# Keys' maxima by a product with the identity, large px in quarters, and one more step in each attention unit, in a fused attention and MoE kernel

## The chip, the cores and the metric

One core of a Trainium2 chip runs the program. The metric is the time of one execution on the device in microseconds; less is better.

## The reference

Linear attention with two softmaxes, then a feed-forward layer with a hard swish. Batch 8, 8 heads, 576 tokens, head size 64; 4608 tokens of 512 features in all, hidden size 2048; everything is float32.

```
q_s = softmax(q, over the 64 features);  k_s = softmax(k, over the 576 tokens)
kv  = k_s^T v                 # 64 x 64 for each batch and head
x   = q_s kv                  # tokens x 512 when the heads stand side by side
h   = x @ w_in;  g = h * clip(h + 3, 0, 6) / 6;  out = g @ w_out
```

## The kernel before

The 4608 tokens are three blocks of 512 ("block 0, 1, 2") and three large blocks of 1024 ("large block 0, 1, 2"). Heads are taken in four pairs `hp`. Each float32 factor of the big products is split into two parts, hi and lo (`split`, L119: a cast on ScalarE, a subtraction on VectorE), and a product is made of three.

**Blocks.** For each of the 16 chunks of the hidden size, `gemm1` makes 12 matmuls of 512 columns (`ph`), `relu6` and `split` make its `g`, and `gemm2` of the chunk before follows, 12 matmuls into four accumulators (`po`). `store` (L701) sends a block's result through the ring of tiles `v`. In block 0 the weights are decoded (`decode`).

**Sums of weights.** The large blocks use a scheme of seven products instead of eight, which needs sums of weight blocks. `sum_weights` (L426) makes four of them for each of 8 pairs of chunks and both sides, so 16 times, one yield or two each, during blocks 1 and 2. The four sums stand in one tile `v`, their hi and lo parts go into two tiles of the ring `gp`, and from there to DRAM (`keep`).

**Large blocks.** `factors(s)` makes the seven right factors from x (L494 on), `phase1` 56 slots of six matmuls into g, `phase2` 56 slots of six for the output. The left factors come from DRAM by `fetch`, through two fixed tiles and the ring `gp` (4 tiles, which `gemm1` uses too).

**Attention.** `token_attention` (L341) is a generator, one per head pair, for block 2 (`block_attention`) and the large blocks (`sb_attention`). Its steps:

1. load q, and for every new batch b: `kt` (keys with features on partitions, one buffer), `ke` (keys with tokens on partitions), `vt`;
2. for every new b the maxima `km` of `kt` (VectorE, L355), spread to 128x128 as `kb` on GpSimd (L357); then q's softmax and its turn into `qT` (`q_softmax_t`; the tile is called m);
3. for every new b: `pm`, a transpose of `kb` on TensorE, so that every row holds the maxima of the keys' features; `ke - pm` (VectorE, L364), its exp (ScalarE);
4. nothing; 5. `kv_of`: ten products of 65 columns, each into one half of the array's columns, give `pkv`, and VectorE makes `kv` from it: 128x128, the two heads on the diagonal, zero elsewhere;
6. for each chunk of 512 tokens `px`: `kv` times `qT`, one product of full size for each batch in the chunk, and a copy into x on ScalarE (L385).

`steps(units, length)` strings the units together: one step per call, a unit's last step behind the first of the next one. The loop over chunks calls it twice a chunk (once for the last two chunks of a block), the large blocks once every two slots. A block's loop runs the attention of the next block, block 2's that of large block 0, and large block s that of s + 1.

`pm`, `pkv` and `px` share two PSUM banks (`bank_a`). From block 1 on TensorE's instructions stay in the order in which the program makes them (`mm`, L85); the other engines' order is the scheduler's, by a timeline of its own. `behind(units)` (L124) makes an exception: what a unit issues comes behind the instructions in `front`, on their engines.

Of the kernel before, what the change touches and what calls it, by code (L numbers as in the profile page):

```python
# [1 line left out]

# [16 lines left out]
P = 128  # L19
# [13 lines left out]
def attention_moe(  # L33
# [88 lines left out]
    front = []  # L122

    def behind(units, count=1):  # L124

        with ExitStack() as order:
            for ins in front:
# [129 lines left out]
    def attention(j, hp):  # L257

        if not j:
            kt, qt, qT, vt, ke = first[hp]  # L260
        else:
            kt, ke, vt = load_k(j, hp)
# [26 lines left out]
    def load_k(b, hp, tokens=False):  # L289
        kt = att.tile([P, S], F32, name="kt", bufs=1)  # L290
        nc.sync.dma_start(kt, kT[b, hp])
        ke = att.tile([P, NCH, P], F32, name="ke", bufs=2)
        if tokens:
            nc.sync.dma_start(ke, k[b, hp].rearrange("p c h d -> p c (h d)"))
        vt = att.tile([P, NCH, 2, D + 1], F32, name="vt", bufs=2)
        nc.sync.dma_start(vt, v[b, hp])
        return kt, ke, vt
# [43 lines left out]
    def token_attention(t0, n, hp, put):  # L341
# [8 lines left out]
        loads = {b: load_k(b, hp, tokens=True) for b in need if (b, hp) not in kvs}  # L350
        yield
        new = {}
        for b, (kt, ke, vt) in loads.items():
            km = att.tile([P, 1], F32, name="km", bufs=2)
            nc.vector.tensor_reduce(km, kt, axis=AX.X, op=ALU.max)  # L355
            kb = att.tile([P, P], F32, name="kb", bufs=2)
            nc.gpsimd.tensor_copy(kb, km.broadcast_to([P, P]))  # L357
            new[b] = ke, vt, kb
        qT = q_softmax_t(qt)
        yield  # L360
        for ke, vt, kb in new.values():
            pm = bank_a("pm")
            flip(pm[:, 0:P], kb)
            nc.vector.tensor_sub(  # L364
                ke, ke, pm[:, 0:P].rearrange("p (o n) -> p o n", o=1).broadcast_to([P, NCH, P])
            )
            nc.scalar.activation(ke, ke, AF.Exp)
        yield
        yield
        for b, (ke, vt, kb) in new.items():  # L370
            kv_of(b, hp, ke, vt)
        yield
        for c in range(n // TB):
            px = bank_a("px")
            at = t0 + c * TB
            for b in need:
                lo, hi = max(b * S - at, 0), min((b + 1) * S - at, TB)
                if lo < hi:
                    mm(px[:, lo:hi], kvs[b, hp], qT[:, c * TB + lo : c * TB + hi], True, True)
            put(c, hp, px)  # L380
        yield

    def sb_attention(s):
        def put(c, hp, px):
            nc.scalar.copy(x_of(s)[:, hp, c * TB : (c + 1) * TB], px)  # L385

        return [token_attention(START + s * SB, SB, hp, put) for hp in (0, 2, 1, 3)]

    def block_attention(j):
        def put(c, hp, px):  # L390
# [35 lines left out]
    def sum_weights(pair, side):  # L426
# [13 lines left out]
        s1, s2, s3, s4 = (sums[:, n * HT : (n + 1) * HT] for n in range(4))  # L440
# [4 lines left out]
        for i in range(2):  # L445
            dst = moe.tile([P, 2, TB], F32R, name="gp", bufs=4).rearrange("p i n -> p (i n)")
            four = dst.rearrange("p (k e n) -> p k e n", k=2, e=2)
            src = sums[:, i * TB : (i + 1) * TB].rearrange("p (k n) -> p k n", k=2)
            split(four[:, :, 0], four[:, :, 1], src)
            for k_ in range(2):  # L450
                block = (S1, S2, S3, S4)[2 * i + k_]
                keep(pair, side, block, dst[:, k_ * TB : (k_ + 1) * TB].bitcast(F32))
# [70 lines left out]
    def relu6(g, r, h):  # L523
        nc.scalar.activation(r, h, AF.Relu, bias=three, scale=1.0)  # L524
        nc.vector.scalar_tensor_tensor(g, r, 6.0, h, op0=ALU.min, op1=ALU.mult)  # L525

    def phase1(s):
        xb, yb, zb = {}, {}, {}
        for i, (p, n) in enumerate(SLOTS1):
# [24 lines left out]
            with tc.high_priority():  # L554
                if n == 1:
                    nc.scalar.copy(h11, x)
# [3 lines left out]
                if n == 3:  # L560
                    nc.scalar.copy(h21, x)
                if n == 2:
                    nc.scalar.copy(h22, y)
                if n == 4:
                    nc.vector.tensor_add(h22, h22, x)  # L565
                if n == 5:
                    relu6(h12, temp(), x)
                if n == 6:
# [3 lines left out]
                    nc.vector.tensor_sub(h12, h22, h12)  # L572
            yield

    def phase2(s):
# [6 lines left out]
        def make():  # L582
# [7 lines left out]
            front[:] = split(t[:, 0], t[:, 1], src)  # L590
# [78 lines left out]
    def gemm1(j, f):  # L669
# [11 lines left out]
        split(gp[:, 0], gp[:, 1], g)  # L681
# [85 lines left out]
    for j in range(NB):  # L767
        if j == 1:
            in_order.append(True)
        if j < NB - 1:  # L770
            turned = (j + 1) * TB >= TURNED
            units = block_attention(j + 1) if turned else [attention(j + 1, hp) for hp in range(NP)]
            step = steps(units, 6 if turned else 4)
        else:
            step = steps(sb_attention(0), 6)
            fac = factors(0)
        chunks = [*range(NFC)] if j < NB - 1 else [NFC - 1, *range(NFC - 1)]
        for n, f in enumerate(chunks):
# [10 lines left out]
            for _ in range((2 if f % 4 == 3 else 1) if not j else 2 if n < 14 else 1):  # L789
# [3 lines left out]
            if j == NB - 1 and n >= 14:  # L793
                for _ in range(3):
                    next(fac, None)
# [7 lines left out]
    with tc.high_priority():  # L803
        for _ in fac:
            pass
        fetch(GROUPS - 2)

    for s in range(NS):
        more = s + 1 < NS
        step = steps(sb_attention(s + 1), 6) if more else iter(())  # L810
# [76 lines left out]
```

## Time and profile before

| | us |
|---|---|
| median of 3 runs (841.83 to 843.0) | 841.92 |
| profiled execution | 839.71 |
| its span in the profile | 837.9 |
| end of block 2, start of large block 0 in it | 346.5 |

TensorE is busy for 96% of the span, VectorE for 81%, ScalarE for 53%, GpSimd for 8%. Times are in us from the start of the span unless ns stands beside them. PE is TensorE, PEld its weight loads, DVE VectorE, ACT ScalarE, POOL GpSimd, SP SyncE. A name like `px<-m,kv` is output <- inputs. A float32 product leaves two records on TensorE, a product of split parts and a transpose one.

### The profile page before, as it was taken

The numbers are of one execution on the slowest core, as the hardware profiler recorded it, in microseconds if no ns is written. First come the engines' busy times: TensorE is split into PE (matmuls) and PEld (weight loads), VectorE is DVE, ScalarE is ACT, GpSimd is POOL, SyncE is SP. The second block draws the span as 40 slices with busy tenths as digits, with TensorE's granted clock in tenths as the row PEclk, the third lists the DMA queues.
The fourth block names the chain that finished last, engine by engine and source line by source line (L and its number), as shares of the span: only waits on it lengthen the run. The fifth ranks groups of instructions, "written<-read, shape, count | busy, mean of one in ns | idle before, by whom it ended". The sixth has DMA issues, their size and how long they took to land.

```text
span 837.9 us, 11778 instructions
## 1 busy us (share of the span) xinstructions
PE 805.7 (96%) x4032; PEld 648.1 (77%) x4032; DVE 677.7 (81%) x1095; ACT 442.4 (53%) x717; POOL 68.0 (8%) x179
## 2 busy tenths in 40 slices
PE   4999989999999999999999999999999999999997
PEld 3677767777887877787877788777888888888886
DVE  7998999999778998579989994698599836558873
ACT  7997764444344454355456653545466535445542
POOL 5000011020100112001112000010000000000000
PEclk9899999999999999999999999999999999999999
DMA  9999676678549661578775577665566775665672
GB/s 362 415 407 319 220 256 208 217 241 288 183 153 357 203 236 51 179 264 292 279 252 184 184 233 254 220 224 162 176 194 188 246 247 187 194 201 187 192 227 98
DMA packets 75643, 192.30 MB, mean 230 GB/s; under 512 B 7232, under 2 KB 19520, under 8 KB 73536
## 3 DMA queue, kind: packets, MB, share of 16 engines
q1 hardware_dynamic: 75008, 190.51, 67.2%
q10 hardware_dynamic: 576, 1.05, 0.4%
q8 instruction: 32, 0.52, 0.3%
q14 instruction: 27, 0.22, 0.1%
HBM read 147.49 MB, written 44.04 MB: 229 GB/s over the span
## 4 chain that ended last, share of the span: by engine, by line
PE 67%; DVE 18%; DMA 5%; ACT 4%; issue 3%; POOL 2%; SPq 0%; ACTq 0%; DVEq 0%; POOLq 0%
PE x L87 30%; PE z L87 12%; PE y L87 11%; PE po L87 6%; PE ph L87 5%; PE px L87 2%; DVE gp L120 2%; POOL swap L312 2%; DVE g L525 2%; PE pkv L87 1%; DVE v L150 1%; DVE v L154 1%; DMA v<-whole 1%; DMA qt<-in_qf_dram 1%; ACT qt L228 1%
## 5 line engine op out<-in xcount | busy, mean ns | idle before, releaser
L120 ACT CAST gf<-g 128x512 fp32r<-128x512 f32 x168 | 104.4, 623 | 95.2 <-DVE gf L120 34.9
L87 PE MATMUL po<-w,gp 128*128 128x512 f32 x576 | 146.5, 400 | 4.1 <-ACT gp L120 3.4
L87 PE MATMUL ph<-x,w 128*128 128x512 f32 x576 | 144.1, 398 | 2.9 <-ACT w L120 2.6
L120 DVE TENSOR_TENSOR gf<-g,gf 128x512 fp32r<-128x512 f32 x168 | 112.9, 685 | 26.2 <-ACT gf L120 25.4
L87 PEld LDWEIGHTS po<-w,gp 128*128 128x128 f32 x576 | 106.3, 189 | 32.4 <-ACT gp L120 6.2
L87 PEld LDWEIGHTS ph<-x,w 128*128 128x128 f32 x576 | 108.7, 190 | 27.8 <-ACT w L120 3.5
L87 PE MATMUL x<-right,gp 128*128 128x512 f32 x384 | 94.9, 392 | 0.4 <-DVE g L565 0.4
L87 PE MATMUL x<-gf,gp 128*128 128x512 f32 x384 | 94.0, 390 | 0.4 <-DVE gf L120 0.4
L87 PEld LDWEIGHTS x<-right,gp 128*128 128x128 f32 x384 | 71.7, 188 | 16.4 <-DVE g L565 0.8
L87 PEld LDWEIGHTS x<-gf,gp 128*128 128x128 f32 x384 | 71.8, 188 | 16.1 <-DVE gf L120 0.8
L524 ACT ACTIVATE g<-ph,three 128x512 f32<-128x512 f32 x48 | 32.8, 688 | 69.1 <-PE ph L87 68.7
L524 ACT ACTIVATE v<-g,three 128x1024 f32<-128x1024 f32 x24 | 27.6, 1151 | 39.3 <-DVE g L569 39.3
L87 PE MATMUL y<-right,gp 128*128 128x512 f32 x192 | 48.1, 395 | 0.0
L87 PE MATMUL x<-right,left 128*128 128x512 f32 x192 | 47.7, 391 | 0.0
L87 PE MATMUL x<-gf,left 128*128 128x512 f32 x192 | 47.3, 390 | 0.1
L87 PE MATMUL z<-gf,gp 128*128 128x512 f32 x192 | 46.6, 389 | 0.0
L120 ACT CAST gp<-g 128x512 fp32r<-128x512 f32 x48 | 29.7, 619 | 25.5 <-DVE g L525 25.3
L87 PEld LDWEIGHTS x<-gf,left 128*128 128x128 f32 x192 | 35.9, 188 | 8.2 <-DVE gf L120 0.6
L87 PEld LDWEIGHTS z<-gf,gp 128*128 128x128 f32 x192 | 36.0, 188 | 7.5
L87 PEld LDWEIGHTS y<-right,gp 128*128 128x128 f32 x192 | 35.6, 188 | 8.0 <-issue 0.5
L87 PEld LDWEIGHTS x<-right,left 128*128 128x128 f32 x192 | 35.8, 188 | 7.4
L524 ACT ACTIVATE g<-g,three 128x512 f32<-128x512 f32 x24 | 17.4, 724 | 43.2 <-DVE g L558 43.2
(134 smaller groups left out, 1306.0 us busy)
## 6 DMA issues: line engine op xcount, KB each, us to landing
gp<-wf SPq DMA_DIRECT2D x112, 512.0 KB, 3.4
left<-wf SPq DMA_DIRECT2D x56, 512.0 KB, 3.4
raw<-in_w_dram SPq DMA_DIRECT2D x16, 1024.0 KB, 13.7
wf<-gp SPq DMA_DIRECT2D x64, 256.0 KB, 3.3
wf<-w SPq DMA_DIRECT2D x48, 256.0 KB, 4.3
vt<-in_v_dram SPq DMA_DIRECT2D x28, 325.0 KB, 5.3
kt<-in_kT_dram SPq DMA_DIRECT2D x28, 288.0 KB, 3.2
ke<-in_k_dram SPq DMA_DIRECT2D x24, 320.0 KB, 4.7
```

The source lines that it names most:

```text
L87: nc.tensor.matmul(out, lhsT, rhs, start=start, stop=stop, skip_group_check=goes_on)
L120: return nc.scalar.copy(hi, src), nc.vector.tensor_sub(lo, src, hi.bitcast(F32))
L150: nc.vector.scalar_tensor_tensor(vu, high, 0xC0000000, m, op0=ALU.bitwise_and, op1=ALU.bitwise_or)
L154: nc.vector.tensor_tensor(vu, vu, low, op=ALU.add)
L228: nc.scalar.activation(qs[:, i], qs[:, i], AF.Exp, bias=qm[:, i : i + 1], accum_out=qr[:, i : i + 1],)
L312: nc.gpsimd.tensor_copy(swap[r : r + QD], stat[o : o + QD])
L524: nc.scalar.activation(r, h, AF.Relu, bias=three, scale=1.0)
L525: nc.vector.scalar_tensor_tensor(g, r, 6.0, h, op0=ALU.min, op1=ALU.mult)
```

## The change

- **Maxima.** `kb` and its copy on GpSimd are gone. `pm` is now a product of `km`, broadcast to 128x128, with the identity; the maxima of two new batches go to two parts of one bank.
- **Loads.** `load_k` is cut in two. Step 1 loads the keys of the first new batch alone; the second's follow in a new step behind the first maximum. A unit has one step more, and `steps` gets length 7 instead of 6.
- **px of the large blocks** is made in quarters: 64x64 products for head h and chunk c, from rows of h, into partitions of c, into one bank for each head. Four copies of 64x512 take them to x instead of two of 128x512. Block 2's px is as before.
- **Order.** The attention of large block 0 follows block 2's directly, in block 1's loop (`chain`), and two steps are called in every chunk. The factors of large block 0 come at chunks 13, 14 and 15 of block 2, two each, behind those chunks' relu and split (`ahead` notes the last such instruction of each engine in `front`); the last one and the fetches have no high priority any more.
- **Sums** are split in place: S1 and S2 go from `sums` into `w4`, S3 and S4 within `sums`. `store` uses the ring `gp` instead of `v`.

```diff
+    def split_ahead(hi, lo, src):
+        for ins in split(hi, lo, src):
+            ahead(ins)
-    front = []
+    front = {}
+    def ahead(ins):
+        front[ins.ins.engine] = ins
+        return ins
...
 def token_attention(t0, n, hp, put):
...
-        loads = {b: load_k(b, hp, tokens=True) for b in need if (b, hp) not in kvs}
-        yield
-        new = {}
-        for b, (kt, ke, vt) in loads.items():
+        new = [b for b in need if (b, hp) not in kvs]
+        def greatest(kt):
             km = att.tile([P, 1], F32, name="km", bufs=2)
             nc.vector.tensor_reduce(km, kt, axis=AX.X, op=ALU.max)
-            kb = att.tile([P, P], F32, name="kb", bufs=2)
-            nc.gpsimd.tensor_copy(kb, km.broadcast_to([P, P]))
-            new[b] = ke, vt, kb
+            return km
+        kt = [load_kt(b, hp) for b in new[:1]]
+        ke, vt = [], []
+        for b in new:
+            ke.append(att.tile([P, NCH, P], F32, name="ke", bufs=2))
+            nc.sync.dma_start(ke[-1], k[b, hp].rearrange("p c h d -> p c (h d)"))
+            vt.append(load_v(b, hp))
+        yield
+        km = [greatest(t) for t in kt]
+        kt = [load_kt(b, hp) for b in new[1:]]
+        yield
+        km += [greatest(t) for t in kt]
         qT = q_softmax_t(qt)
         yield
-        for ke, vt, kb in new.values():
-            pm = bank_a("pm")
-            flip(pm[:, 0:P], kb)
+        pm = bank_a("pm")
+        for i, t in enumerate(km):
+            mm(pm[:, i * P : (i + 1) * P], t.broadcast_to([P, P]), ident, True, True, True)
...
 def sb_attention(s):
-        def put(c, hp, px):
-            nc.scalar.copy(x_of(s)[:, hp, c * TB : (c + 1) * TB], px)
+        def put(t0, hp, need, qT):
+            px = [bank_a("px") for _ in range(2)]
+            rows = [slice(h * D, (h + 1) * D) for h in range(2)]
+            for both in zip_longest(*(segments(need, t0 + c * TB) for c in range(2))):
+                for c, part in enumerate(both):
+                    if part:
+                        b, lo, hi = part
+                        for h, r in enumerate(rows):
+                            mm(px[h][rows[c], lo:hi], kvs[b, hp][r, r],
+                               qT[r, c * TB + lo : c * TB + hi], True, True, True)
+            for c in range(2):
+                for h, r in enumerate(rows):
+                    nc.scalar.copy(x_of(s)[r, hp, c * TB : (c + 1) * TB], px[h][rows[c]])
...
 def sum_weights(pair, side):
-        s1, s2, s3, s4 = (sums[:, n * HT : (n + 1) * HT] for n in range(4))
+        s1, s3, s2, s4 = (sums[:, n * HT : (n + 1) * HT] for n in range(4))
...
-        for i in range(2):
-            dst = moe.tile([P, 2, TB], F32R, name="gp", bufs=4).rearrange("p i n -> p (i n)")
...
+        to, of = (t.rearrange("p (k e n) -> p k e n", k=2, e=2) for t in (w4, sums))
+        split(to[:, :, 0].bitcast(F32R), to[:, :, 1].bitcast(F32R), of[:, :, 0])
+        split(of[:, :, 0].bitcast(F32R), of[:, :, 1].bitcast(F32R), of[:, :, 1])
...
 def store(j, po):
-            ob = moe.tile([P, 2 * DM], F32, name="v", bufs=3)[:, 0:DM]
+            if t % 2 == 0:
+                two = moe.tile([P, 2, TB], F32R, name="gp", bufs=4).bitcast(F32)
+            ob = two[:, t % 2]
...
-            step = steps(units, 6 if turned else 4)
+            step = steps(units, 7 if turned else 4)
+            if j == NB - 2:
+                step = chain(step, steps(sb_attention(0), 7))
...
-            for _ in range((2 if f % 4 == 3 else 1) if not j else 2 if n < 14 else 1):
+            for _ in range((2 if f % 4 == 3 else 1) if not j else 2):
                 next(step, None)
...
-            if j == NB - 1 and n >= 14:
-                for _ in range(3):
-                    next(fac, None)
+            if j == NB - 1:
+                behind(fac, {13: 2, 14: 2, 15: 2}.get(n, 0))
...
-    with tc.high_priority():
-        for _ in fac:
-            pass
-        fetch(GROUPS - 2)
+    behind(fac, 7)
+    fetch(GROUPS - 2)
```

`segments(need, at)` gives for a chunk the batches in it with their first and last column.

## Rows read from the trace of the kernel before

**Rows 1.** The page, parts 1 and 2: busy us of each engine (share of the span) and number of instructions; then the span in 40 slices, busy tenths, and the granted clock of TensorE in tenths.

```profile
PE 805.7 (96%) x4032; PEld 648.1 (77%) x4032; DVE 677.7 (81%) x1095; ACT 442.4 (53%) x717; POOL 68.0 (8%) x179
...
PE   4999989999999999999999999999999999999997
...
PEclk9899999999999999999999999999999999999999
```

**Rows 2.** Stretches, from the middle of block 1's first chunk on: start and end, length, busy us (and instructions) of each engine, granted clock, share and rate of the DMA engines.

```profile
142.00:209.00 67.00, 65.40 (x352) 51.58 (x351) 62.94 (x138) 29.80 (x50) 9.53 (x28) 1.00 0.73 244
209.00:237.00 28.00, 28.00 (x125) 23.20 (x124) 21.35 (x35) 11.18 (x18) 4.35 (x16) 1.00 0.42 147
237.00:346.00 109.00, 105.25 (x596) 84.70 (x595) 91.00 (x156) 49.21 (x74) 14.64 (x40) 1.00 0.59 201
346.00:437.00 91.00, 90.55 (x536) 73.20 (x535) 74.86 (x127) 46.08 (x71) 9.40 (x32) 1.00 0.80 272
437.00:494.00 57.00, 56.04 (x245) 45.22 (x244) 56.05 (x84) 34.18 (x54) 6.25 (x8) 1.00 0.60 190
```

**Rows 3.** The chain of waits in large block 1, in order of time: start, us, what and how many records.

```profile
528.53 1.36 PE y L87 x6
529.89 0.73 PE pkv L87 x20
530.62 1.58 PE y L87 x6
532.20 2.74 PE x L87 x12
...
536.31 1.83 PE px L87 x6
538.14 2.77 PE x L87 x12
540.91 0.11 PE pm L93
...
543.77 2.72 PE x L87 x12
...
552.91 1.85 PE px L87 x6
```

**Rows 4.** Waits of TensorE's matmuls from 142 us on: who waited for whom, us in total, times, longest.

```profile
PE pm L93 <- ACT x L385: 1.4, 1, 1.4
PE px L87 <- DVE m L330: 1.3, 1, 1.3
PE po L87 <- ACT gp L120: 1.2, 2, 0.9
PE pm L93 <- DVE ke L364: 1.0, 1, 1.0
PE po L87 <- DVE gp L120: 0.5, 2, 0.3
PE px L87 <- DVE kv L206: 0.4, 2, 0.3
PE x L87 <- DVE g L565: 0.4, 1, 0.4
PE x L87 <- DVE gf L120: 0.4, 1, 0.4
```

**Rows 5.** The chain of waits, two units of large block 0's and 1's attention and two chunks of block 1: start, us, what.

```profile
228.86 2.72 PE po L87 x12
231.58 2.72 PE ph L87 x12
...
367.41 1.75 PE px L87 x8
...
395.73 1.32 PE pkv L87 x40
...
402.72 1.73 PE px L87 x8
```

**Rows 6.** TensorE in order of time in block 2: start, us, engine, line, operation, output <- inputs, shapes, number [idle before it <- releaser].

```profile
257.73 1.89 PE L87 MATMUL px<-m,kv 128*128 128x192 f32 x8
259.52 0.30 PE L93 MATMUL pm<-ident,kb 128*128 128x128 f32 x1
261.19 0.30 PE L93 MATMUL pm<-ident,kb 128*128 128x128 f32 x1 [1.37 <-ACT x L385]
```

**Rows 7.** Groups of instructions: line, engine, operation, output <- inputs, shapes, number | busy us, mean ns of one | idle before them and what ended it.

```profile
L120 DVE TENSOR_TENSOR gp<-v,gp 128x512 fp32r<-128x512 f32 x32 | 21.3, 685 | 0.0
L120 ACT CAST gp<-v 128x512 fp32r<-128x512 f32 x32 | 18.9, 618 | 9.3 <-DVE v L444 5.0 <-DVE v L442 3.9 <-DMA wf<-gp 0.5
L364 DVE TENSOR_TENSOR ke<-ke,pm 128x640 f32<-128x640 f32 x24 | 18.9, 805 | 1.8 <-PE pm L93 1.7
L355 DVE TENSOR_REDUCE km<-kt 128x1 f32<-128x576 f32 x24 | 17.9, 744 | 4.5 <-DMA kt<-in_kT_dram 4.4
L320 DVE TENSOR_REDUCE qm<-qt 128x32 f32<-128x1024 f32 x12 | 14.6, 1218 | 9.6 <-DMA qt<-in_qf_dram 9.6
L385 ACT COPY x<-px 128x512 f32<-128x512 f32 x24 | 13.3, 588 | 1.1 <-PE px L87 0.7
L206 DVE SCALAR_TENSOR_TENSOR kv<-pkv,rk,mask 128x128 f32<-128x128 f32 x32 | 10.8, 341 | 0.2
L357 POOL COPY kb<-km 128x128 f32<-128x128 f32 x24 | 9.7, 416 | 222.6 <-PE pm L93 185.6 <-DVE km L355 34.6 <-DVE rk L203 2.5
L254 ACT COPY ke<-pe 64x128 f32<-64x128 f32 x4 | 1.0, 259 | 0.8 <-PE pe L93 0.8
```

**Rows 8.** The page, part 6: DMA issues, output <- input, queue, number, KB each, median us from issue to landing.

```profile
wf<-gp SPq DMA_DIRECT2D x64, 256.0 KB, 3.3
...
kt<-in_kT_dram SPq DMA_DIRECT2D x28, 288.0 KB, 3.2
```

**Rows 9.** VectorE in order of time at the end of block 2, columns as in rows 6.

```profile
340.73 1.22 DVE L328 TENSOR_TENSOR qt<-qt,qr 128x1024 f32<-128x1024 f32 x1
341.87 0.68 DVE L525 SCALAR_TENSOR_TENSOR g<-g,ph 128x512 f32<-128x512 f32 x1
```

More of the change, by code (lines that the diff above doesn't have):

```diff
@@ L1 @@
 from contextlib import ExitStack
+from itertools import chain, zip_longest
 import numpy as np
@@ L368, in token_attention @@
+        for i, t in enumerate(km):
+            mm(pm[:, i * P : (i + 1) * P], t.broadcast_to([P, P]), ident, True, True, True)
+        for i, t in enumerate(ke):
+            most = pm[:, i * P : (i + 1) * P]
+            most = most.rearrange("p (o n) -> p o n", o=1).broadcast_to([P, NCH, P])
+            nc.vector.tensor_sub(t, t, most)
+            nc.scalar.activation(t, t, AF.Exp)
         yield
         yield
-        for b, (ke, vt, kb) in new.items():
-            kv_of(b, hp, ke, vt)
+        for b, *two in zip(new, ke, vt):
+            kv_of(b, hp, *two)
@@ L372, in token_attention, with segments @@
         yield
[L373 to L380, printed above, removed]
+        put(t0, hp, need, qT)
         yield
+    def segments(need, at):
+        parts = [(b, max(b * S - at, 0), min((b + 1) * S - at, TB)) for b in need]
+        return [x for x in parts if x[1] < x[2]]
@@ L387, in sb_attention, with put @@
         return [token_attention(START + s * SB, SB, hp, put) for hp in (0, 2, 1, 3)]
     def block_attention(j):
-        def put(c, hp, px):
+        def put(t0, hp, need, qT):
+            px = bank_a("px")
+            for b, lo, hi in segments(need, t0):
+                mm(px[:, lo:hi], kvs[b, hp], qT[:, lo:hi], True, True)
             x_hi, x_lo = x_block(j)
@@ L444, in sum_weights @@
         nc.vector.tensor_sub(s4, a12, s2)
-        for i in range(2):
-            dst = moe.tile([P, 2, TB], F32R, name="gp", bufs=4).rearrange("p i n -> p (i n)")
[L447 to L452, printed above, removed]
+        to, of = (t.rearrange("p (k e n) -> p k e n", k=2, e=2) for t in (w4, sums))
+        split(to[:, :, 0].bitcast(F32R), to[:, :, 1].bitcast(F32R), of[:, :, 0])
+        split(of[:, :, 0].bitcast(F32R), of[:, :, 1].bitcast(F32R), of[:, :, 1])
+        for t, blocks in ((w4, (S1, S2)), (sums, (S3, S4))):
+            for n, block in enumerate(blocks):
+                keep(pair, side, block, t[:, n * TB : (n + 1) * TB])
         yield
@@ L555, in phase1 @@
                 if n == 1:
-                    nc.scalar.copy(h11, x)
+                    ahead(nc.scalar.copy(h11, x))
                 if n == 0:
@@ L802, in attention_moe @@
         pass
-    with tc.high_priority():
-        for _ in fac:
-            pass
-        fetch(GROUPS - 2)
+    behind(fac, 7)
+    fetch(GROUPS - 2)
     for s in range(NS):
         more = s + 1 < NS
-        step = steps(sb_attention(s + 1), 6) if more else iter(())
+        step = steps(sb_attention(s + 1), 7) if more else iter(())
         fac = factors(s + 1) if more else iter(())
```

44 lines of the change are left out of this document (24 added, 20 removed).

## The prediction

> **What bounds the kernel now.** I read the page first. TensorE is busy 805.7 of 837.9 us, and its row of slices is nines from the second slice on, at a granted clock of 0.9 and more [rows 1]. Busy time alone does not say how tight the stream is, so next I read the chain of waits as a list of pieces. Twelve matmuls of 512 columns take 2.72 us there, again and again, with no idle piece between them; an attention product simply pushes the next ones back [rows 3]. From the start of block 1 on, every microsecond of attention on TensorE is therefore a microsecond of the kernel, and what else can be won is TensorE's waits. Third view: those waits from 142 us on. They are few: 2.4 us before the maxima's products, 1.3 us for a turned q, 0.4 for a kv, 1.7 us of gemm2 on its split, 0.8 us on g and gf in the large blocks [rows 4]; 6.6 us in all. Last I read the stretches, to see which engine would be next. VectorE is full from 142 to 209 us (62.9 of 67.0) and from 437 to 494 (56.1 of 57.0); elsewhere it has room; ScalarE is near half everywhere [rows 2].
>
> **Large px in quarters.** Removed: for each of 12 units (4 head pairs, 3 large blocks) two chunks of 512 columns through a full 128x128 array whose off-diagonal half is zero. Their pieces are 1.73 to 1.85 us [rows 3, 5]; I take 1.76 as the mean, 12 x 1.76 = 21.1 us. The eight-record pieces of 1.73 and 1.75 give 1.74 / 1024 = 1.70 ns a column for this number format.
> Added: per unit one product of 64x64 for each head and chunk, on four quadrants of the array. The trace has no quadrant, but it has halves: pkv uses 128x64 column halves, one per head. Forty records (20 products of 65 columns) take 1.32 us and twenty take 0.73, so ten more products cost 0.59 us [rows 3, 5]. One after another they would take 10 x 65 x 1.70 ns = 1.11 us. The two halves thus do overlap. The fixed part is 0.73 - 0.59 = 0.14 us, and the piece behind is 1.58 instead of 1.36 us, another 0.22: 0.36 us for going into the split array and back.
> Bounds. If all four quadrants overlap, each streams 512 columns: 512 x 1.70 = 0.87 us, plus 0.36 = 1.23 us a unit, 12 x 1.23 = 14.8 us, a gain of 6.3 us; with no fixed part 10.4 us, a gain of 10.7. If only two overlap, the time is that of the full array plus the fixed part, 2.10 us a unit, 25.2 us, a loss of 4.1. Strictly one after another (3.48 us of streaming) would lose 25 us, and the halves of pkv exclude it. I take four: the two quadrants of one head are column halves as in pkv, and the row halves write separate banks here.
> The Trainium skill, TensorEngine Tiling (Array Packing), section Key Properties, says that changing the tiling mode drains TensorE, which speaks against short excursions such as these. The trace agrees, with the 0.36 us above; without that drain the gain would be the 10.7 us.
>
> **Evacuation of the quarters.** Four copies of 64x512 replace two of 128x512 (588 ns [rows 7]). The copy of 64x128 took 259 ns [rows 7], so a copy goes mostly by columns: I take 0.59 us for each, at best half of it. That is 24 x 0.59 = 14 us more on ScalarE, which has 442.4 of 837.9 us busy [rows 1]. What is queued behind is the relu and cast of the next chunk; they have the 5.44 us of a gemm2 and a gemm1 (2 x 2.72 [rows 5]) to cover a burst of 2.4 us, so I put it at nothing. Without that cover it would be up to 1.2 us a unit. Both banks of the pair are now held until then; the next user is the maxima's product three steps later.
>
> **Maxima by a product.** Removed: 24 copies on GpSimd of 416 ns [rows 7] and 24 transposes, 0.11 us of the chain each [rows 3]. GpSimd has nothing else due in that time but the swaps of q's statistics, which no longer queue behind it. Added: 24 fp32 products of 128 columns, 128 x 1.70 = 0.22 us. That is +0.11 x 24 = +2.6 us, between nothing (if it costs what the transpose did) and twice that.
> Two maxima now share one bank. Before, in two of the four units of large block 0, the first px, the second px and two pm fought over two banks inside one chunk: the second pm waited 1.37 us on a copy out [rows 6], another time 1.0 us on the subtraction [rows 4]. With seven steps to a unit and two steps to a chunk, px and pm fall into different chunks, and one bank needs no second wait: -2.4 us. What could be late next is the second block's maximum, now one step later, because its keys are fetched only when the first maximum has been taken. The fetch takes 3.2 us on the page's median [rows 8] and a chunk lasts 5.44, so it lands in time.
>
> **Order of the work.** Six steps to a unit instead of five spread the same VectorE work over 13 chunks instead of 11 in block 1; the full stretch 142 to 209 us eases by 1/6 of the attention in it. The px that waited 1.3 us for its turned q [rows 4] is the last of that stretch: I take -0.9. On the other side the first unit of large block 0 now comes into the end of block 1, where VectorE has 28.0 - 21.4 = 6.6 us free [rows 2] for some 10 us of work (five passes of 1.22 for the softmax, two maxima of 0.74, two subtractions of 0.81, two kv of 0.34 [rows 7]); the rest runs into block 2, which has 109 - 91 = 18 us free [rows 2]. I cost it at nothing; without that cover it is 3.3 us.
> The factors at the end of block 2 are pinned behind each chunk's split, over three chunks instead of two. The waits of gemm2 in blocks 1 and 2 are 1.7 us [rows 4]. Ahead of the longest, at the end of block 2, VectorE was in a softmax pass of the next unit (1.22 us) when the relu's product came due [rows 9], and the pin doesn't move that. I take -0.5, between 0 and -1.7. The key loads no longer hold SyncE's queue for the first maximum; no wait of TensorE on a load is among [rows 4], so nothing.
>
> **Sums in place, stores by the other ring.** Sums save nothing in instructions: two casts of 618 ns and two subtractions of 685 [rows 7], 16 times. But they now form a chain: the second cast overwrites what the first subtraction reads. Of the 1.24 us of casts, VectorE waits through none today (idle 0.0 [rows 7]). Other work is there to fill it, so nothing; without the cover it is 16 x 1.24 = 20 us of VectorE. Both tiles of a sum are held until their stores land (3.3 us [rows 8]), from a ring of three. The stores of the outputs move to the other ring, which frees as much.
>
> **Sum.** -6.3 + 2.6 - 2.4 - 0.9 - 0.5 = -7.5 us. The profiled execution took 839.7 us around a span of 837.9; the median is 841.9, 2.2 above it. I carry the difference over: 841.9 - 7.5 = 834.4 us.
>
> **Rivals.**
> *Only two quadrants overlap.* fp32 products leave two records each, one behind the other on the same quadrant (8 records for 4 products), so the second pass of one can only run beside the first pass of the next if starts are kept in order. The rate of pkv fits this as well as free overlap; nothing of a row half speaks either way. Then +4.1 instead of -6.3: 834.4 + 10.4 = 844.8 us. It decides once a unit's px, with what it adds to the piece behind, costs over 1.76 + 1.2 / 12 = 1.86 us (1.2 is what the other terms win together).
> The Trainium skill, TensorE: Matmul & The Clock Gate, section Part 3, states that matmuls start and end strictly in program order, by which this case would come; no row here shows it for quadrants.
> *VectorE becomes the bound in block 1.* About 9 of the 16 sums lie in 142 to 209 us; 9 x 1.24 = 11.2 us of chained casts against 4.1 us of room [rows 2], so 7 us late, and the moved unit is 3.3 us over its room. TensorE takes px and pkv in program order and waits for them: 834.4 + 10.4 = 844.8 us. For it: that stretch is full already. Against it: other work, of the relu and of attention, already stands between the operations of a sum. It decides when TensorE's waits on VectorE and ScalarE in blocks 1 and 2 grow by more than the 7.5 us won.
> *More is won:* the drain is hidden, and the waits of the large blocks go too (0.8, and 0.4 on a kv): 834.4 - 4.4 = 830 us.
>
> **Chances and range.** Forecast 0.52, two quadrants 0.20, VectorE 0.15, more 0.13. The range from 829 to 845 takes in nearly all of the forecast and of "more", most of "two quadrants" and half of "VectorE", about 0.8. Faster by over 0.2% (1.7 us, about what a measurement of this kernel can tell from no change): 0.64; within: 0.11; slower: 0.25.
>
> **What would show it.** In the chain after, a unit's px piece near 0.9 to 1.0 us with 0.2 behind it; 2.0 says that two overlap. A pm pair near 0.45 us. No wait of pm on ScalarE or VectorE. Waits of TensorE on VectorE in 142 to 346 us below 2 us; the casts of the sums without idle VectorE ahead of their subtractions. The prediction is wrong if quadrants don't overlap by heads, or if attention is late for TensorE's fixed order.

## The result, and the profile after

The changed kernel takes 846.51 us in the median (844.11 to 847.46, 8 runs), the kernel before 841.88 in the same session (839.77 to 843.12, 8 runs). The ratio is 1.0054, 95% interval 1.0038 to 1.0070: slower by half a per cent, where 0.9% faster was forecast. The profiled execution took 846.66 us around a span of 844.9. That is 7.0 us over the span of before; the medians are 4.6 apart, since the profiled execution of before lies 2.2 below its median.

From the first matmul of each stage to the first of the next, in us of the two traces (block 0 from the start of the span, large 2 to its end):

| | block 0 | block 1 | block 2 | large 0 | large 1 | large 2 |
|---|---|---|---|---|---|---|
| before | 136.6 | 100.2 | 109.5 | 169.6 | 164.5 | 157.5 |
| after | 136.1 | 107.1 | 107.8 | 171.9 | 164.5 | 157.5 |

So block 1 loses 6.9 us and large block 0 another 2.3; block 2 wins 1.7; large block 1, where four units of quarters should have won 2.1, wins nothing.

First the stretches after, with columns as in [rows 2]; the borders are moved with the later stages.

```profile
142.00:209.00 67.00, 65.29 (x336) 52.64 (x337) 57.07 (x123) 27.85 (x46) 7.60 (x24) 1.00 0.63 217
209.00:244.00 35.00, 32.72 (x189) 26.47 (x188) 30.97 (x57) 15.68 (x25) 5.23 (x16) 0.95 0.68 232
244.00:351.00 107.00, 103.32 (x591) 82.42 (x590) 80.05 (x142) 50.66 (x77) 9.11 (x32) 0.98 0.47 165
351.00:442.00 91.00, 87.93 (x565) 70.02 (x564) 77.21 (x130) 51.16 (x78) 7.93 (x24) 1.00 0.83 285
```

In the stretch that was full, VectorE now does 57.1 us of work instead of 62.9, and 123 instructions instead of 138. Block 1 is longer and VectorE is emptier: it does not lack room, it stands and waits. The clock, 1.00 in all stretches of [rows 2], is 0.95 and 0.98 in two of these.

Next TensorE's waits from 142 us on, as in [rows 4].

```profile
PE pkv L88 <- ACT ke L390: 3.7, 3, 2.1
PE x L88 <- DVE g L605: 2.9, 4, 1.1
PE po L88 <- DVE gp L121: 2.8, 2, 1.7
PE x L88 <- DMA gp<-wf: 1.4, 1, 1.4
PE po L88 <- ACT gp L121: 1.3, 2, 0.9
```

Of the waits of [rows 4], those of pm and of px on m are gone, as forecast. In their place stand keys' exponentials, g and gp, and a weight fetch: 13.0 us with the small ones, against 6.6.

The chain in large block 1, columns as in [rows 3]:

```profile
532.56 1.36 PE x L88 x6
533.91 0.22 PE pm L88 x2
534.14 1.39 PE x L88 x6
...
543.32 2.72 PE x L88 x12
546.03 1.10 PE px L88 x10
...
548.44 4.58 DMA qt<-in_qf_dram
...
554.18 0.69 DVE g L605
...
554.91 3.03 PE x L88 x12
```

A unit's quarters take 1.10 us of the chain; the twelve matmuls of y behind them start over 2.86 us (546.99 to 549.85) where 2.72 is usual. That makes 1.16 us, where a unit of before made 1.88 (1.83, and 0.05 on the twelve behind it [rows 3]). With only two quadrants at a time the streaming alone would take 1.74 us, at the 1.70 ns a column of before: more than two run side by side. A maximum's product (two records) costs 0.22. Both prices are near the forecast, the first a little better than the 1.23. But the chain no longer runs in matmuls alone: it now goes through the fetch of the next q and a g.

**The stall in block 1.** VectorE in order of time, columns as in rows 6:

```profile
207.01 0.43 DVE L482 TENSOR_TENSOR v<-v 128x256 f32<-128x256 f32 x1 [2.62 <-DMA wf<-v]
...
208.14 0.43 DVE L485 TENSOR_TENSOR v<-v 128x256 f32<-128x256 f32 x1
209.55 1.22 DVE L332 TENSOR_REDUCE qm<-qt 128x32 f32<-128x1024 f32 x1 [0.99 <-DMA qt<-in_qf_dram]
210.69 0.81 DVE L389 TENSOR_TENSOR ke<-ke,pm 128x640 f32<-128x640 f32 x1
```

ScalarE at the same time:

```profile
208.14 0.62 ACT L121 CAST v<-v 128x512 fp32r<-128x512 f32 x1 [5.08 <-DVE v L483]
208.67 0.69 ACT L564 ACTIVATE g<-ph,three 128x512 f32<-128x512 f32 x1
211.53 0.74 ACT L390 ACTIVATE ke<-ke 128x640 f32<-128x640 f32 x1 [2.18 <-DVE ke L389]
```

And TensorE:

```profile
203.75 1.52 PE L88 MATMUL ph<-x,w 128*128 128x512 f32 x6
...
208.09 2.88 PE L88 MATMUL ph<-x,w 128*128 128x512 f32 x12
212.32 0.80 PE L88 MATMUL pkv<-vt,ke 128*64 128x65 f32 x20 [1.35 <-ACT ke L390]
214.06 4.59 PE L88 MATMUL po<-w,gp 128*128 128x512 f32 x12 [0.94 <-ACT gp L121]
```

Read from the top: the first addition of a sum (L482) writes a tile of the v ring. That tile was a w4 which the sum before had split in place, and its store to wf has not landed. VectorE stands 2.62 us. The sum's cast stands at the head of ScalarE's queue 5.08 us, and the relu of the chunk (L564) comes behind it at 208.67, though its ph was done at about 205.3. VectorE goes on with q and keys, all late; pkv and po wait. Then the twelve po take 4.43 us (214.06 to 218.49, where the next ph starts) instead of 2.72. The granted clock over these 2 us stretches, columns as in rows 2, says why:

```profile
212.00:214.00 2.00, 0.80 (x20) 0.66 (x20) 2.00 (x5) 1.48 (x4) 0.00 (x0) 1.00 1.01 283
214.00:216.00 2.00, 1.94 (x5) 1.55 (x6) 2.00 (x4) 1.30 (x3) 0.00 (x0) 0.51 0.85 292
216.00:218.00 2.00, 2.00 (x7) 1.62 (x6) 0.91 (x4) 0.98 (x2) 0.00 (x0) 0.63 1.03 365
```

After standing 1.35 us, 0.80 us of pkv and standing 0.94, TensorE was granted 0.51, its 1.2 GHz level, and was back at 1.00 from 218 on. That adds 1.7 us to 2.3 of waiting. With the 2.0 us of waits at 142 to 145 us, block 1 has 6.0 us of such loss; the version below with the sums and the stores as before has none, and its block 1 is 6.8 shorter.

### The profile page after: what moved, and what is told of

Read it like the earlier page. It is cut to its first block, busy times and chain, and to the rows that moved or that the text cites. A ratio compares the mean times of both kernels' runs of the same rounds, so it can differ in the third digit from the quotient of the medians.

```text
span 844.9 us, 11935 instructions
## 1 busy us (share of the span) xinstructions
PE 805.4 (95%) x4144; PEld 645.6 (76%) x4144; DVE 676.1 (80%) x1095; ACT 459.6 (54%) x741; POOL 60.2 (7%) x155
## 4 chain that ended last, share of the span: by engine, by line
PE 56%; DVE 20%; DMA 12%; issue 4%; ACT 4%; POOL 2%; SPq 0%; ACTq 0%; DVEq 0%; POOLq 0%
PE x L88 27%; PE z L88 11%; PE y L88 10%; DMA qt<-in_qf_dram 4%; DMA wf<-v 3%; PE po L88 3%; PE ph L88 2%; DVE g L565 2%; POOL swap L324 2%; PE px L88 2%; DVE v L121 1%; DVE v L160 1%; DMA kt<-in_kT_dram 1%; DVE gp L121 1%; DVE v L164 1%
## 5 line engine op out<-in xcount | busy, mean ns | idle before, releaser
L88 PE MATMUL po<-w,gp 128*128 128x512 f32 x576 | 149.4, 406 | 6.6 <-ACT gp L121 3.5
L88 PEld LDWEIGHTS po<-w,gp 128*128 128x128 f32 x576 | 108.2, 193 | 35.4 <-ACT gp L121 6.1
L88 PEld LDWEIGHTS ph<-x,w 128*128 128x128 f32 x576 | 107.4, 188 | 28.9 <-ACT w L121 4.0
L564 ACT ACTIVATE g<-ph,three 128x512 f32<-128x512 f32 x48 | 32.9, 687 | 40.2 <-PE ph L88 39.8
L324 POOL COPY swap<-qm 32x32 f32<-32x32 f32 (+1 forms) x64 | 21.4, 335 | 347.6 <-DVE qm L332 345.6
L564 ACT ACTIVATE v<-g,three 128x1024 f32<-128x1024 f32 x24 | 27.7, 1155 | 29.4 <-DVE g L609 29.4
```

What stands on the lines that cost most here:

```text
L88: nc.tensor.matmul(out, lhsT, rhs, start=start, stop=stop, skip_group_check=goes_on)
L324: nc.gpsimd.tensor_copy(swap[r : r + QD], stat[o : o + QD])
L564: ahead(nc.scalar.activation(r, h, AF.Relu, bias=three, scale=1.0))
```

## The experiments

Medians in us; each ratio is to the kernel before in the same session (841.55 to 842.67) with its 95% interval.

**Undo the sums and the stores, or the order.** u_sums is the changed kernel with

```diff
-        split(to[:, :, 0].bitcast(F32R), ...)   # S1, S2 into w4
-        split(of[:, :, 0].bitcast(F32R), ...)   # S3, S4 in place
+        for i in range(2):                      # each into a tile of gp, as before
+            dst = moe.tile([P, 2, TB], F32R, name="gp", bufs=4)...
...
-            ob = two[:, t % 2]                  # store(): gp ring
+            ob = moe.tile([P, 2 * DM], F32, name="v", bufs=3)[:, 0:DM]
```

> The changed kernel with the sums' split through the ring gp and the stores of blocks 0 to 2 through the ring v again, as before; all else as changed. Theory A (the sums held in the ring v until their stores land make VectorE wait at the head of its queue, 7.4 us in all on those stores in the trace after, and relu, exp and with them TensorE come late in blocks 1 and 2): 840 to 842 us, and the fetch of large block 0 that waited 1.4 us for a store in the ring gp is in time. Theory B (the order of the work, the moved unit and the pinned factors, costs it): 845 to 847 us, no change.

u_order keeps these, takes the first large block's attention out of block 1, unpins the factors and gives the last of them and the fetches high priority again:

```diff
-            if j == NB - 2:
-                step = chain(step, steps(sb_attention(0), 7))
...
-                behind(fac, {13: 2, 14: 2, 15: 2}.get(n, 0))
+            if j == NB - 1 and n >= 14:
+                for _ in range(3):
+                    next(fac, None)
...
+    with tc.high_priority():
```

> The changed kernel with large block 0's attention in block 2 alone and the factors of large block 0 unpinned, in chunks 14 and 15 and with high priority, as before; steps keep length 7. Theory B (the moved unit and the pin make VectorE wait for q's transfer, 10.8 us in block 2 in the trace after against 1.1 before): 841 to 843 us, and that wait below 4 us. Theory A: 845 to 848 us, the waits on the sums' stores remain.

Measured: u_sums 838.36, 0.9955 (0.9932 to 0.9979); u_order 847.24, 1.0056 (1.0038 to 1.0074). The loss, and more than it, is in the sums and stores; the order is not its cause. The longest of TensorE's waits in u_sums, 136 to 346 us:

```profile
PE px L88 <- DVE kv L216: 1.2, 1, 1.2
PE po L88 <- ACT v L748: 1.0, 1, 1.0
...
```

They are 3.3 us in all, against 7.8 in the changed kernel; block 1 takes 100.3 us.

**Which of the two.** u_sums1 undoes the first half of that diff alone, u_store1 the second.

> The changed kernel with the sums' split through the ring gp again; the stores of blocks 0 to 2 stay in the ring gp as changed. If the sums held in the ring v until their stores land are the cause: 838 to 840 us, VectorE without a wait on those stores, and only the late fetch at the start of large block 0 (1.4 us) left of the loss. If the stores' ring is: 845 us or more.

> The changed kernel with the stores of blocks 0 to 2 through the ring v again; the sums stay in place. If the sums are the cause, the ring v is now shared by both: 846 to 850 us, no better than the changed kernel. If the stores' ring is the cause: 839 to 841 us.

Measured: u_sums1 839.65, 0.9971 (0.9950 to 0.9993); u_store1 842.33, 0.9991 (0.9973 to 1.0009). The second lies between the two expectations. From the changed kernel's 1.0054, undoing the sums alone wins 0.83% (7.0 us), undoing the stores alone 0.63% (5.3), both 0.99% (8.3): each half has a share, and the two overlap.

The profiles say the same of block 1: 107.1 us in the changed kernel, 105.6 with the stores undone, 103.2 with the sums undone (a profiled execution 2.3 above its median), 100.3 with both. The stores' share lies mostly in TensorE's wait of 2.0 us at the start of the block. It stands in u_sums1 too,

```profile
PE po L88 <- DVE gp L121: 2.2, 1, 2.2
```

and is 0.3 us or nothing from 136 to 160 us in every kernel whose stores go through v. By the code the next sum there has to wait for tiles of v that the stores take. With the stores in gp the ring v is free, and the next sum starts earlier. VectorE puts its weights together (L473) at 136.66 us in the changed kernel, and in u_sums, where the stores' multiplications come first (L746), at 150.23. The first three lines are of the changed kernel, the last two of u_sums:

```profile
136.66 1.29 DVE L473 TENSOR_TENSOR v<-w 128x512 f32<-128x512 f32 x2
143.04 0.41 DVE L482 TENSOR_TENSOR v<-v 128x256 f32<-128x256 f32 x1
143.71 0.69 DVE L121 TENSOR_TENSOR gp<-g,gp 128x512 fp32r<-128x512 f32 x1
...
145.37 0.68 DVE L746 TENSOR_SCALAR v<-po 128x512 f32<-128x512 f32 x1
150.23 1.29 DVE L473 TENSOR_TENSOR v<-w 128x512 f32<-128x512 f32 x2
```

In the changed kernel additions of that sum (L482) stand ahead of the splits of g that gemm2 waits for.

In large block 0 the changed kernel and u_sums1, with the stores in the gp ring, take 171.9 and 171.7 us, u_store1 and u_sums without them 169.8 and 170.5. The chain of the changed kernel shows one place:

```profile
354.32 4.91 DMA out_dram<-gp
...
359.25 4.50 DMA gp<-wf
...
363.88 1.62 PE x L88 x6
```

A weight fetch takes a gp tile that still holds an output on its way out; TensorE waits 1.4 us for it here and 0.3 in u_sums1. u_order, with these stores too but its fetches at high priority, has no such wait and takes 170.1 us. The rest of the difference is not explained, and neither is all of the overlap of the two halves.

**What of the sums in place.** The prediction's rival had the chain of cast and subtraction. Four kernels part it, all with the stores as before; w4 holds the weights that a sum reads, sums the four sums:

```
u_store1      S1, S2 to w4           then S3, S4 in place in sums
c1            S1, S2 to a gp tile    then S3, S4 in place in sums
c2            S1, S2 to w4           then S3, S4 to a gp tile
c3_cast_late  S3, S4 to a gp tile    then S1, S2 in place in sums
c5_tile_held  S1, S2 to a gp tile    then S3, S4 to w4
```

c1 as a diff; the others move the same lines:

```diff
-        split(to[:, :, 0].bitcast(F32R), to[:, :, 1].bitcast(F32R), of[:, :, 0])
+        gp = moe.tile([P, 2, TB], F32R, name="gp", bufs=4).rearrange("p i n -> p (i n)")
+        into = gp.rearrange("p (k e n) -> p k e n", k=2, e=2)
+        split(into[:, :, 0], into[:, :, 1], of[:, :, 0])
...
-        for t, blocks in ((w4, (S1, S2)), (sums, (S3, S4))):
+        for t, blocks in ((gp.bitcast(F32), (S1, S2)), (sums, (S3, S4))):
```

> The changed kernel with the stores of blocks 0 to 2 in the ring v, and of the two splits of a sum the first one into a tile of the ring gp: w4 is free at once, and what is left in place is the second split, whose cast waits for the first subtraction. Block 1 took 105.6 us with both splits in place and 100.3 with none. If the chain (the cast behind the subtraction) costs it: 104 us or more. If the hold of w4 does: 102 or less.

> The other half: the first split goes into w4 as changed, which is held until its stores land, the second into a tile of the ring gp, so that no cast waits for a subtraction. If the chain costs it: block 1 at 101 to 102 us. If the hold of w4 does: 104 us or more.

> The changed kernel with the output stores undone, and the sums laid out so that the first split takes the last two sums, S3 and S4, into a tile of the gp ring, and the second takes S1 and S2 in place: w4 is free as soon as the four sums stand, but the first cast must still wait for the last sum. Theory A (the cast waits in ScalarE's queue, in order, for a late operation of VectorE, and the chunk's relu stands behind it): block 1 stays near 106 us and the time near 843 us. Theory B (w4 is held until its stores land, so the ring of three gives no tile): block 1 falls to about 101 us and the time to about 839 us.

> The other half of the pair: the first split takes S1 and S2 into a tile of the gp ring, so its cast is due after the second sum, and the second split takes S3 and S4 into w4, which is so held until its stores land. Theory A (the cast's wait for the last sum): block 1 near 101 us, about 839 us. Theory B (the hold of w4): block 1 near 106 us, about 843 us. Both fast would say that wait and hold are needed together.

| | chained second split | first cast waits for the last sum | w4 held till its stores land | median | ratio |
|---|---|---|---|---|---|
| u_sums | no | no | no | 838.36 | 0.9955 (0.9932 to 0.9979) |
| c1 | yes | no | no | 839.09 | 0.9958 (0.9937 to 0.9979) |
| c3_cast_late | yes | yes | no | 838.60 | 0.9963 (0.9945 to 0.9981) |
| u_store1 | yes | yes | yes | 842.33 | 0.9991 (0.9973 to 1.0009) |
| c2 | no | yes | yes | 844.02 | 1.0018 (0.9997 to 1.0040) |
| c5_tile_held | no | no | yes | 843.19 | 1.0014 (0.9997 to 1.0031) |

The column that parts them is the third: three kernels that hold w4 take 842.3 to 844.0, three that don't 838.4 to 839.1. By the ratios c2 and c5_tile_held are clear of all three; u_store1's interval just meets theirs. Neither the chain nor the late cast costs anything that shows. Block 1 agrees for c1 (101.0 us) and c2 (106.8), which are alike but for which split goes where. The waits of the first additions on a store (wf<-v) part less sharply: 10.3 us in u_store1, 2.2 in c2, 2.0 in c5_tile_held, none in u_sums and c3_cast_late, but 2.5 in c1, once, in block 2. Waits on the next weights (v<-whole) are no sign, since p_order below, without the hold, has 6.1 us of them. c3_cast_late has

```profile
DVE v L482 <- DMA v<-whole: 3.0, 3, 1.1
```

and c5_tile_held

```profile
DVE v L482 <- DMA v<-whole: 7.0, 3, 3.9
DVE v L482 <- DMA wf<-v: 2.0, 1, 2.0
```

The ring of three explains why w4 and not sums, which c1 and c3_cast_late hold as long: after w4, sums and the next w4, the next sums takes the first w4's tile at once, while the old sums tile is wanted only by the sum after that. This order is read from the code. In its one profile c5_tile_held loses mostly in block 2 (102.9 and 110.0 us against 102.2 and 107.3 in c3_cast_late), in no one wait, and less than its median says; block 1 did not come near the 106 us expected. What the hold costs, 3 to 5 us, rests on the medians, and how it gets to TensorE was followed in one stall alone, the one above.

v4g3 is the changed kernel with a longer v ring, paid with a shorter one for gp:

```diff
-... name="v", bufs=3  ... name="gp", bufs=4 ... GROUP, GROUPS = 2, 6
+... name="v", bufs=4  ... name="gp", bufs=3 ... GROUP, GROUPS = 2, 5
```

> The changed kernel with four tiles in the ring v and three in the ring gp (the fetch keeps five groups ahead instead of six); the sums stay in place. If it is the hold of the tiles until the stores land, a fourth tile takes VectorE's waits on those stores from 7.4 us to under 2, and the time from the start of block 1 to the end of block 2 falls from 214.9 us by 4 or more. If it is the chain of two casts and two subtractions itself, those waits fall but the 214.9 us stay. The large blocks may lose by the shorter ring.

Measured: 852.68, 1.0118 (1.0091 to 1.0145). VectorE's waits on the sums' stores fell from 7.4 to 2.2 us, but 8.9 us of waits on the next weights (v<-whole) came, blocks 1 and 2 stayed at 215.5 us (214.9 in the changed kernel), and large block 0 lost 6 to the shorter ring. By its expectation this outcome speaks for the chain and against the hold. But the kernel waits for other things in place of the stores, and its gp ring, which gemm2 needs too, is shorter, so it decides neither; against the chain stand c1 and c3_cast_late. A longer ring at that price doesn't mend the sums in place.

**Quarters, product and order.** o_px is the kernel before with the quarters alone, o_pxpm with the product in one bank too; both with the steps of before.

```diff
-            px = bank_a("px")
-            mm(px[:, lo:hi], kvs[b, hp], qT[:, ...], True, True)
+            px = [bank_a("px") for _ in range(2)]
+            mm(px[h][rows[c], lo:hi], kvs[b, hp][r, r], qT[r, ...], True, True, True)
```

> The kernel before with the quartered px of the large blocks alone. If TensorE bounds and the four quadrants overlap: a unit's px falls from 1.76 to 1.1 us, 12 units, 842 - 7 = 835 us, give or take 2 for what the schedule does. If the evacuation by four copies or the two banks held at once cost as much as the quarters win: 840 to 843 us.

> The kernel before with the quartered px and with the maxima by a product into one bank, six steps to a unit as before. By the terms of the forecast -6.3 + 2.6 - 2.4: 836 us. If the product's 2.6 us are not made up by the waits on the bank, 838 us; slower than px alone by 2 to 3 us then.

Measured: 845.71, 1.0046 (1.0022 to 1.0069), and 845.44, 1.0034 (1.0011 to 1.0057). Both lie above all that was expected of them. o_px wins 2.3 and 2.4 us in large blocks 0 and 1, about four units at 0.65 each, and loses 7.2 in block 2. There the maxima stand in the same chunk as the quarters and need their banks, which four copies must empty first:

```profile
258.60 1.09 PE L88 MATMUL px<-m,kv 64*64 64x192 f32 x16
...
263.10 0.30 PE L94 MATMUL pm<-ident,kb 128*128 128x128 f32 x1 [3.41 <-ACT x L401]
```

From u_sums, p_px takes the quarters out, p_pm the product, p_pxpm both, so that only the order is left; p_order takes out the moved unit and the pinned factors, with the diff of u_order, and keeps the seven steps and the loads apart.

```diff
 # p_px, p_pxpm
-            px = [bank_a("px") for _ in range(2)]
...
+            for c in range(2):
+                px = bank_a("px")
...
+                nc.scalar.copy(x_of(s)[:, hp, c * TB : (c + 1) * TB], px)
 # p_pm, p_pxpm
-            mm(pm[:, i * P : (i + 1) * P], t.broadcast_to([P, P]), ident, True, True, True)
...
+            nc.gpsimd.tensor_copy(kb, km.broadcast_to([P, P]))
...
+            pm = bank_a("pm")
+            flip(pm[:, 0:P], kb)
```

> The changed kernel with sums and stores as before and with px of the large blocks as full products again: what the quarters are worth in the new order. By the trace (1.1 against 1.76 us a unit, 12 units) it is 6 to 8 us slower than the kernel with sums and stores as before: 838.4 + 7 = 845 us. If the four copies or the two banks held cost something: less than 4 us slower.

> The changed kernel with sums and stores as before, and the maxima by a copy on GpSimd and a transpose into a bank of its own again, in the new order of steps. The product's price in the trace is 0.36 us for two maxima against 0.14 for two transposes: 24 x 0.11 = 2.6 us. If nothing else hangs on it: 838.4 - 2.6 = 836 us. If the copy on GpSimd or the second bank brings a wait back: 838 to 841 us.

> The changed kernel with sums and stores undone and the order too: the first large block's attention in block 2 only, the factors unpinned. What stays is quarters, product and the units of six yields with the loads apart. If the moved unit and the pinned factors carry the 3.5 us that the version without the sums' part wins over the kernel before: about 842 us. If the spread of the steps in the small blocks carries them: about 838.5 us, block 2 near 107.5 us.

> The changed kernel with sums and stores, quarters and product all undone, so that only the order of the work is left (six yields to a unit, loads apart, the unit in block 1, pinned factors). If the order alone carries what is won: 837.5 to 838.5 us. If quarters and product win something together that neither wins alone: 840 us or more.

| | quarters | product | moved unit, pinned factors | median | ratio |
|---|---|---|---|---|---|
| u_sums | yes | yes | yes | 838.36 | 0.9955 (0.9932 to 0.9979) |
| p_px | no | yes | yes | 838.97 | 0.9960 (0.9943 to 0.9978) |
| p_pm | yes | no | yes | 837.56 | 0.9954 (0.9938 to 0.9971) |
| p_pxpm | no | no | yes | 837.65 | 0.9942 (0.9919 to 0.9964) |
| p_order | yes | yes | no | 841.64 | 0.9994 (0.9975 to 1.0014) |

The order wins all there is to win: the four with it stand 3.2 to 4.6 us under the kernel before. Quarters and product win nothing with it; without the moved unit and the pins they win nothing either (p_order), and with six steps to a unit they lose (o_px, o_pxpm). The fastest, p_pm and p_pxpm, are 0.5% under the kernel before and 1% under the changed one; no run tells them from u_sums.

Where the order wins is seen in p_order against u_sums. p_order's block 1 is 2.0 us shorter, without the moved unit (98.3 against 100.3), its block 2 4.9 us longer (112.2 against 107.4). The longest of TensorE's waits there are

```profile
PE po L88 <- ACT gp L121: 3.6, 1, 3.6
PE pkv L88 <- ACT ke L390: 2.1, 1, 2.1
...
```

6.5 us in all, against 3.3 in u_sums. The wait of 3.6 us is at the end of block 2: from 329.5 to 334.1 us VectorE makes four operations of the unpinned factors, and only then the product of a relu that was done at 329.57.

Where the quarters' gain goes is seen, in part, in u_sums against p_px: blocks 1 and 2 equal (207.7 and 207.6), large block 1 2.1 us shorter, large block 0 1.8 us longer. TensorE's wait on g from 346 us on is in u_sums

```profile
PE x L88 <- DVE g L606: 3.2, 4, 1.2
```

and in p_px, where the line is L593,

```profile
PE x L88 <- DVE g L593: 1.1, 1, 1.1
```

That is 2.1 us of some 7.8 (12 units at 0.65); the rest is not accounted for. In o_px, with six steps to a unit, no such wait is in the list, and the gain in the large blocks stays.

**Steps behind g.** The wait on g has q's reduction ahead of it on VectorE, so p_behind pins each attention step of the large blocks of u_sums behind the slot's evacuation:

```diff
-                next(step, None)
+                behind(step)
```

> The changed kernel with sums and stores as before, and the attention's steps in the large blocks pinned behind that slot's evacuation on each engine. There VectorE stood in the first pass over q, waiting for q's transfer, with a sum of g behind it for which TensorE waited (3.2 us in 4 places). If that order is what takes back the quarters' gain: those waits fall below 1 us and the time from 838.4 to 834 to 836 us. If VectorE is short of time in large block 0 and not merely of order, the waits move to px and pkv, and the time stays at 838 to 841.

Measured: 857.35, 1.0183 (1.0158 to 1.0208). The wait on g is gone, and these are there instead:

```profile
PE px L88 <- DVE m L342: 10.3, 3, 6.8
PE pm L88 <- DVE km L366: 7.0, 3, 3.2
```

Here attention done ahead of its time in VectorE's gaps is worth more than a g in time. The waits moved to other products, as the second expectation had it, but the time is 16 us over it.

## Why the prediction was wrong, by its steps

The step that failed is the last of the forecast, sums in place and stores by the other ring, put at nothing: undoing both wins 8.2 us (846.51 to 838.36) and turns the sign. The gain of the quarters is the second that did not come. The steps follow in the forecast's order.

**Quarters.** The price was right: 1.10 to 1.16 us a unit against 1.23 forecast and 1.76 before, and the copies of 64x512 take 583 ns as forecast. The rival of two quadrants falls; it needed 1.86. The Trainium skill, TensorE: Matmul & The Clock Gate, section Part 3, states that matmuls start and end strictly in program order. The prediction set this beside its rival of 2.10 us a unit; the trace, with its 1.10, shows no such loss for four quadrants. What failed is the sentence that every microsecond of attention on TensorE is a microsecond of the kernel. It was read from the trace of before, with 6.6 us of waits. In the large blocks of o_px it still holds; in the new order, with the product shortened, the next g is late four times. In the fence above of the chain, q's DMA lands at 553.02, and VectorE in order:

```profile
553.04 1.22 DVE L332 TENSOR_REDUCE qm<-qt 128x32 f32<-128x1024 f32 x1 [2.30 <-DMA qt<-in_qf_dram]
554.18 0.68 DVE L605 TENSOR_TENSOR g<-g,x 128x512 f32<-128x512 f32 x1
```

The g waits behind a reduction that waits for a transfer. q has one tile, which is free only when the unit before has transposed it. The Trainium skill, TensorE: Matmul & The Clock Gate, section Part 1, calls VectorE's queue strictly first in, first out; the row agrees, with 2.30 us of standing ahead of a g. Of the -6.3 the changed kernel kept none that a run could show; the late g accounts for about 2 of it, the rest stays open.

**Maxima.** +0.11 us a product and no more waits of pm: the terms +2.6 and -2.4 are right in size in the trace. The -2.4 belongs to the steps: p_pm, with a bank for each maximum, waits 0.3 us for pm, and o_pxpm, with the product and six steps, 7.1. Undoing the product should then have won 2.6; p_pm's ratio is that of u_sums, and where the 2.6 went is not shown.

**Order.** Forecast were -0.9 and -0.5, at most -3, and nothing for the moved unit. Measured by the medians, -3.3 for the moved unit and the pins (p_order to u_sums) and -4.4 for all of the order (the kernel before to p_pxpm). The term was too small. The pins were allowed at most 1.7 us, from the waits of gemm2 in the trace of before; in p_order the one wait at the unpinned factors is 3.6. That the moved unit could win was not considered; no run parts it from the pins.

**Sums in place, stores by the other ring.** This is the step that turned the sign: "Other work is there to fill it, so nothing" and, of the tiles held, "The stores of the outputs move to the other ring, which frees as much." The first was right, as far as c1 and c3_cast_late can tell: the chain costs nothing. The second failed: stores come once per block, sums once per chunk, and what matters is who takes the held tile next. The hold of w4 until its stores land costs 3 to 5 us (the table of six), as VectorE's wait of 2.62 us on wf<-v shows at work in one place. The rival on VectorE named the place and near the size (7 us late in block 1, which is 6.9 longer), but not the cause, a chain of casts against a full engine; and by its own test it does not decide: TensorE's waits in both blocks grew by 2.4 us, not 7.5. The rest came with the slow clock behind them.

"Frees as much" failed for the stores as well. It left out who starts earlier when v is free, the next sum, ahead of block 1's first g (2.0 and 2.2 us of waits), and what the gp ring is for at the end of block 2, the weight fetches of large block 0 (1.4 and 0.3 us).

One sum in the rivals is off: "more is won" adds up to 4.4 + 1.2 = 5.6 us and 828.8 us, not 830; nothing hangs on it.

With the sums and stores undone the forecast's whole sum of -7.5 us should have come; u_sums shows -3.2 (841.55 to 838.36). The quarters' 6.3 are missing, and the order gave more than its 1.4.

## What to carry to other kernels

A tile that is written in place and then stored lives until the store lands: ask which operation takes its buffer next in the ring, on which engine that operation stands at the head of the queue, and what stands behind it. A ring that is freed starts its next user earlier: ask what that then stands ahead of. A shorter product on the engine that bounds the kernel pays only as far as its next operand is early; read that slack before booking the gain. When several edits come together, cost the one that "saves nothing" as carefully as the one that saves: here it decided the sign, and the order of the work, booked at 1.4 us, was worth more than the faster product.

## What the runs showed of the hardware

64x64 quadrants with fp32 data run side by side: a unit's products on four of them take 1.10 us, where the two full-array products over the same columns take 1.83 [rows 3]. A copy out of 64 partitions takes as long as one of 128 (583 and 588 ns for 512 columns [rows 7]). A stall can cost more than its length: after 1.35 and 0.94 us of standing close together TensorE ran at 0.51 and 0.63 of its clock over 4 us, and lost 1.7 us more; after a stand of 2.11 us at 259 to 261 us it was granted 0.50:

```profile
262.00:264.00 2.00, 2.00 (x22) 1.79 (x23) 2.00 (x5) 1.33 (x3) 0.00 (x0) 0.50 1.05 392
```

It need not. In p_order TensorE stood 3.64 us from 331.83 on and 0.80 soon after, and the clock stayed at 1.00, as it did in the changed kernel after the 2.0 us at 142 to 145 us. What makes the difference is not shown.

```profile
332.00:334.00 2.00, 0.00 (x0) 0.00 (x0) 2.00 (x2) 1.51 (x2) 1.96 (x2) 1.00 0.04 14
...
336.00:338.00 2.00, 1.59 (x7) 0.94 (x5) 2.00 (x3) 0.35 (x2) 0.00 (x0) 1.00 0.00 0
```
